# Loading x of the first four chunks one token per partition, with another order of steps

## The chip, the cores and the metric

The kernel runs on one core of one Trainium2 chip. The metric is the device time in microseconds of one execution; three executions of the kernel before took 118.48, 118.60 and 118.94 us (median 118.6). A profile of one execution shows the five engines: TensorE (PE; its weight loads are shown as PEld), VectorE (DVE), ScalarE (ACT), GpSimd (POOL) and SyncE (SP, which here only issues DMA transfers).

## What is computed

Two layers, one after the other. The first is a gated scan over a sequence (batch 4, heads H = 8, sequence S = 768, head size D = 32, state size N = 16); the second is a feed-forward layer with a GELU of the tanh form on the 3072 tokens of 256 values that the first gives (hidden size 2048). The reference of the first layer, cut to its core (its chunks are 32 long; the result doesn't depend on that):

```python
la = log_a[:, :, sl]; cum = np.cumsum(la, axis=-1)
L = np.exp(cum[:, :, :, None] - cum[:, :, None, :]) * causal
M = np.einsum('bhin,bhjn->bhij', Cc, Bc) * L
y_intra = np.einsum('bhij,bhjd->bhid', M, xc)
y_inter = np.einsum('bhin,bhnd->bhid', Cc, state) * np.exp(cum)[..., None]
y[:, :, sl] = y_intra + y_inter
decay_from_j = np.exp(cum[:, :, -1:] - cum)
Bx = np.einsum('bhjn,bhjd->bhjnd', Bc, xc) * decay_from_j[..., None, None]
state = np.exp(np.sum(la, axis=-1))[..., None, None] * state + np.sum(Bx, axis=2)
```

and of the second:

```python
x = attn_out.transpose(0, 2, 1, 3).reshape(B * S, H * D)
h = x @ w_in
g = 0.5 * h * (1 + np.tanh(np.sqrt(2 / np.pi) * (h + 0.044715 * h ** 3)))
out = g @ w_out
```

## The kernel before, in words

The sequence of each batch is cut into six chunks of 128 tokens, 24 in all; two chunks form a unit u (0 to 11), and a unit is also a tile of 256 tokens for the second layer. The kernel is a list of small named steps. Each step has an engine and a function that issues its instructions (`add`, L751); the string ORDERED (L17) lists all of them in the order in which they are issued. Each engine works through its own instructions in that order, so the list settles what stands behind what on every engine and on the DMA queues of SP and ACT. A letter after a colon picks the engine (A, D, P), `~n` issues n blocks of 128 columns of matmuls with zeros on TensorE (`fill`, L701), and `+n` puts n such blocks ahead of a step s1. Waits between engines follow from the data and from the buffers; every DMA transfer also waits for the transfer issued eight before it.

The steps that matter here, by name:

- Loads: load_aq and load_a (the gate a, once for the first four chunks of batch 0 and once for all), load_bc0 (C and B of the first four chunks, L149), load_bc1 (the last two of batch 0), load_bc (other batches), load_x.u (L171, two transfers of 128 KB, one token per partition: runs of 32 floats), load_wi.q and load_wo.q (quarters of the two weights, 512 KB each), and load_x4 (L182), which loads x of the first four chunks of batch 0 in one transfer with four successive tokens per partition.
- The gate: clipq, Rq (a scan), tpq, recip0, peq, ppq, pendq for the first four chunks; clip, R, tp2, tp6.q, recip, recip1, pe, pp, pend for all batches. They give the factors rt, pt and the decays pend.
- B and C: mulb and mulc multiply them by their factors, with four tokens per partition; tw.i transposes, ew copies the result back in token order as bh0 and ce0. For batch 1 that is mul, T, E, and F splits C by head; N turns B back to tokens on the partitions and bn copies it. Batches 2 and 3 go through DRAM instead (load_wr, load_tr, load_bn).
- x of units 0 and 1: with four tokens per partition it must be put back in token order. x4 casts it, XX (L563) multiplies it by a selection matrix unp (set up by c_unp) into the order of tokens, and xn copies the outcome. XD (L575) forms the products of B and x straight from the loaded order, r by r. Other units: castx.u casts x to bf16, and D.u multiplies B (bn) and x.
- Per unit: G.u (products of B and C), M.u.i (L612, times the mask, 1024 columns on VectorE; for unit 0 half of it as GE on ACT and ME on GpSimd), S (the state of a chunk), SP (the state spread over heads), Y.u (both parts of y, which needs M, x and SP), yev.u (copies y as the input of the second layer). From u = 3 on, Y.u also issues D and G of the next unit.
- The second layer: s1.u.i (eight steps a unit of four matmuls each, L708), gelu.u.i on ACT, s2.chunk.quarter (four steps a chunk of four matmuls each, L725), oev (copies the sum), store. wi.q.k and wo.q.k cast the loaded weights. s1 needs yev of its unit and w_in; s2 needs the gelu steps and w_out.

For unit 0 the list before runs: a, C and B of four chunks, x4, w_in; tw, ew, G.0, M.0.0, XX.0, XD.0, SP.0, Y.0, yev.0, and then the first s1 with unit 1's steps in between.

Of the kernel before, what the change touches and what calls it, by code (L numbers as in the profile page):

```python
# [8 lines left out]
FP32 = mybir.dt.float32  # L9
# [12 lines left out]
load_wi.2 SP.0 ~17 Y.0 wi.0.1:A wi.0.0:A S.0.0 yev.0.0.2 wi.1.1 XX.1 wi.1.0:A R XD.1 S.0.1
load_wi.3 S.1.0 s1.0.0 SP.1 xn.2 load_bc1.1 wi.2.0 gelu.0.0 G.1 s1.0.1 s1.0.2 M.1.1 M.1.0
load_bc1.0 load_wo.0 wi.3.0:D gelu.0.1 wi.2.1 s1.0.3 load_x.2 SP.2 pe wi.3.1 gelu.0.2 load_bc.1.1
gelu.0.3 tp6.2 s1.0.4 load_bc.1.0 gelu.0.4 load_x.3 load_wo.1 xn.3 s1.0.5 s1.0.6 Y.1 gelu.0.5 pp
tp2 gelu.0.6 tp6.3 recip1 s1.0.7 S.1.1 yev.1.0.2 mul1.0:P mul1.1:P tp6.1 pend gelu.0.7 s1.1.0
wo.0.1 T1.0 s1.1.1 T1.1 gelu.1.0 bh1 N1 gelu.1.1 s1.1.2 tp6.0 s1.1.3+10 bn1 ce1.1 load_wo.2
castx.2.None SP.3 wo.0.0 ce1.0 gelu.1.2 gelu.1.3 G.2 s1.1.4 recip.1.4 s1.1.5 gelu.1.4 M.2.1
mul.1.1:P s2.0.0.0.o D.2 M.2.0 load_x.4 gelu.1.5 s2.0.1.0.o s1.1.6 T.1.1 gelu.1.6 S.2.0 s1.1.7
# [954 lines left out]
```

## Time and profile before

| what | us |
|---|---|
| three runs | 118.48, 118.60, 118.94 |
| span of the profiled execution, first to last instruction | 116.9 |
| median of the runs less that span | 1.7 |
| TensorE busy | 110.1 |
| ScalarE busy | 72.1 |
| VectorE busy | 69.4 |
| GpSimd busy | 21.4 |
| start of the first s1 (L717) | 12.50 |
| last copy out (L323) starts | 113.91 |

The profile gives the span of the profiled execution; its own time outside the span isn't listed, so the median of the runs is set beside it. Busy times are sums over the whole span. TensorE is busy nearly throughout, but its matmuls with zeros (7.6 us in 23 instructions at L705) count as busy too. The granted TensorE clock is full in every slice. 15.97 MB move by DMA, and the DMA engines are nearly full from about 4 to 34 us and then have room.

### The profile page before, as it was taken

What the parts mean: (1) busy time and instruction counts of PE and PEld (TensorE: products, weight loads), DVE (VectorE), ACT (ScalarE), POOL (GpSimd) and SP (SyncE); (2) the same over time, 40 slices, a digit from 0 to 9 for tenths busy, and PEclk for the clock granted to TensorE, in tenths of its full rate; (3) what the DMA queues carried; (4) which work ended last, traced back from release to release, by engine and by line L of the source; (5) the groups of instructions that cost most, each with busy time, mean ns of one, the idle gap of its engine ahead of it and who ended that gap; (6) DMA issues with size and microseconds to landing.
All of it is one profiled execution on the core that took longest, in us unless ns stands there. A gap on an engine that the chain in (4) does not pass through costs nothing.

```text
span 116.9 us, 3379 instructions
## 1 busy us (share of the span) xinstructions
PE 110.1 (94%) x1426; PEld 92.0 (79%) x1426; DVE 69.4 (59%) x140; ACT 72.1 (62%) x139; POOL 21.4 (18%) x38
## 2 busy tenths in 40 slices
PE   6988999998899999999999999999999999999990
PEld 2354676776789979989898999889798998999970
DVE  5898899899785936716695583049493462101020
ACT  2249899968486459565766677828465587447501
POOL 7606816908206000052200000000000000000000
PEclk9999999999999999999999999999999999999999
DMA  0999997999983929998407472044201201101113
GB/s 26 228 332 357 281 252 178 208 288 257 305 143 90 185 47 219 213 253 200 72 25 171 121 163 63 0 140 98 40 6 63 71 0 52 43 0 50 45 47 132
DMA packets 43007, 15.97 MB, mean 137 GB/s; under 512 B 36657, under 2 KB 41457, under 8 KB 42993
## 3 DMA queue, kind: packets, MB, share of 16 engines
q1 hardware_dynamic: 42800, 15.64, 56.0%
q8 instruction: 11, 0.18, 0.6%
q10 hardware_dynamic: 192, 0.13, 0.5%
q14 instruction: 4, 0.02, 0.1%
HBM read 11.04 MB, written 3.93 MB: 128 GB/s over the span
## 4 chain that ended last, share of the span: by engine, by line
PE 75%; DMA 8%; DVE 6%; SPq 6%; issue 2%; POOL 1%; ACT 0%; DVEq 0%; POOLq 0%
PE o_ps L735 33%; PE hp L717 30%; DMA bcf<-in_B_dram 8%; PE yb L735 3%; SPq L190 3%; PE ga L603 3%; PE yb L658 2%; DVE m L613 2%; PE yb L667 2%; DVE ce L523 1%; SPq L150 1%; DVE bh L327 1%; DVE bc L484 1%; SPq L159 1%; SPq L183 1%
## 5 line engine op out<-in xcount | busy, mean ns | idle before, releaser
L721 ACT ACTIVATE gT<-hp 128x512 bf16<-128x512 f32 x96 | 54.3, 596 | 25.0 <-PE hp L717 24.6
L717 PE MATMUL hp<-xm,w_in_sb 128*128 128x256 bf16 x384 | 53.3, 273 | 0.6 <-ACT gT L721 0.4
L735 PE MATMUL o_ps<-w_out_sb,gT 128*128 128x256 bf16 x352 | 47.3, 273 | 0.0
L717 PEld LDWEIGHTS <-w_in_sb 128*128 128x128 bf16 x384 | 41.4, 114 | 3.5 <-issue 1.9
L735 PEld LDWEIGHTS <-gT 128*128 128x128 bf16 x384 | 37.0, 98 | 4.9 <-issue 1.1
L327 DVE COPY o_sb<-o_ps 128x256 f32<-128x256 f32 x13 | 5.5, 425 | 23.8 <-PE o_ps L735 20.4
L613 DVE TENSOR_TENSOR m<-ga,tri 128x1024 bf16<-128x1024 f32 x12 | 14.6, 1218 | 0.1
L613 DVE TENSOR_TENSOR m<-gb,tri 128x1024 bf16<-128x1024 f32 x11 | 13.4, 1219 | 0.7 <-PE gb L603 0.7
L323 ACT ACTIVATE o_sb<-o_ps 128x256 f32<-128x256 f32 x9 | 3.5, 385 | 9.2 <-PE o_ps L735 9.2
L705 PE MATMUL yb<-wz 128*128 128x512 bf16 (+3 forms) x23 | 7.6, 481 | 1.1 <-DVE wz L220 1.1
L691 DVE SCALAR_TENSOR_TENSOR sp_new<-s_new,pend,bmask 128x256 bf16<-128x256 f32 x17 | 7.9, 476 | 0.0
L327 DVE CAST xm<-yb 128x512 bf16<-128x512 f32 x6 | 4.1, 687 | 5.8 <-PE hp L636 4.8
L684 DVE SCALAR_TENSOR_TENSOR s_new<-s_new,pend,hp 128x64 f32<-128x64 f32 x13 | 3.6, 279 | 6.4 <-PE hp L636 6.2
L705 PEld LDWEIGHTS <-wz 128*128 128x128 bf16 x26 | 3.0, 120 | 5.1 <-issue 3.2
L667 PE MATMUL yb<-m,x 128*32 128x128 bf16 x192 | 6.1, 220 | 0.0
L603 PE MATMUL ga<-ce,bh 32*128 32x256 bf16 x48 | 4.7, 273 | 1.3 <-DVE bn L327 0.9
L484 POOL TENSOR_TENSOR bc<-bc_t,pt 128x768 bf16<-128x768 f32 x2 | 3.0, 1494 | 13.8 <-DMA bc_t<-in_C_dram 13.7
L658 PE MATMUL yb<-ce,sp_new 128*32 128x128 bf16 x160 | 5.3, 221 | 0.0
L603 PE MATMUL gb<-ce,bh 32*128 32x256 bf16 x48 | 4.7, 273 | 0.0
L735 PE MATMUL yb<-w_out_sb,gT 128*128 128x256 bf16 x32 | 4.6, 273 | 0.0
L667 PEld LDWEIGHTS <-x 128*32 128x32 bf16 x192 | 3.8, 97 | 0.8 <-issue 0.8
L323 ACT ACTIVATE xm<-yb 128x512 bf16<-128x512 f32 x6 | 3.6, 595 | 1.1 <-PE hp L636 1.1
(115 smaller groups left out, 79.5 us busy)
## 6 DMA issues: line engine op xcount, KB each, us to landing
out_dram<-o_sb SPq DMA_DIRECT2D x24, 128.0 KB, 1.9
x_t<-in_x_dram SPq DMA_DIRECT2D x20, 128.0 KB, 3.9
wf<-in_moe_w_in_dram SPq DMA_DIRECT2D x4, 512.0 KB, 6.7
wf<-in_moe_w_out_dram SPq DMA_DIRECT2D x4, 512.0 KB, 5.5
bc_t<-in_C_dram SPq DMA_DIRECT2D x3, 384.0 KB, 5.8
bc_t<-in_B_dram SPq DMA_DIRECT2D x3, 384.0 KB, 5.5
scr<-bc SPq DMA_DIRECT2D x4, 192.0 KB, 2.2
x_t<-in_x_dram SPq DMA_DIRECT2D x1, 512.0 KB, 5.8
```

What stands on the lines that cost most here:

```text
L323: nc.scalar.activation(o, i, AF.Copy)
L327: nc.vector.tensor_copy(out=o, in_=i)
L484: (nc.gpsimd if eng == "POOL" else nc.vector).tensor_tensor(out=d["bc16"][:, i], in0=d["bc"].rearrange("p i h (r n) -> p i r h n", r=R6)[: ...
L603: nc.tensor.matmul(out=gbank(g)[:, 256 * k:256 * k + 256], lhsT=bh_of(2 * u + k)[gs], rhs=ce_of(2 * u + k)[gs], start=True, stop=True, til ...
L613: nc.vector.tensor_tensor(out=m_of(u)[:, 2 * i:2 * i + 2].rearrange("p g k e t -> p (g k e) t"), in0=gx[i].rearrange("p g (k t) -> p (g k) ...
L658: nc.tensor.matmul(out=y4[32 * j:32 * j + 32, k, w], lhsT=sp[:, 32 * h:32 * h + 32], rhs=ce_of(gc)[:, h % 2], start=first(j), stop=False, ...
L667: nc.tensor.matmul(out=y4[32 * j:32 * j + 32, k, w], lhsT=X16[u][:, k, 32 * h:32 * h + 32], rhs=m[:, h // 2, h % 2, :], start=first(j), st ...
L691: nc.vector.scalar_tensor_tensor(out=sp_new.rearrange("p (g d) -> p g d", g=4), in0=(XN[0][:, H * D:H * D + 64] if gc == 0 else state[("s" ...
L705: nc.tensor.matmul(out=t[:, 0:m * 128], lhsT=wz, rhs=w3.to_broadcast([128, m, 128]), start=True, stop=True, skip_group_check=True)
L717: nc.tensor.matmul(out=hp[:, j * T:(j + 1) * T], lhsT=w_in_k[:, w, q, k], rhs=xm[:, w, u * T:(u + 1) * T], start=(w == 0), stop=(w == 1))
L721: nc.scalar.activation(gts[u][:, 2 * i:2 * i + 2], hps.pop((u, i)).rearrange("p (j t) -> p j t", j=2), AF.Gelu_apprx_tanh)
L735: nc.tensor.matmul(out=ops[gc], lhsT=gts[u][:, fi, k * Q:(k + 1) * Q], rhs=w_out_sb[:, fi, :], start=(fi == 0 and (u > 0 or k == 0)), stop ...
```

## The change

Units 0 and 1 are treated like the others. load_x4, x4, XX, XD, xn and c_unp with its selection matrix go. load_x gets an argument for the chunk, so each unit is two steps, load_x.u.0 and load_x.u.1, each of 128 KB, and units 0 and 1 are loaded by them too: load_x.0.0 and load_x.1.0 right behind C and B of four chunks, load_x.0.1 and load_x.1.1 behind the first quarter of w_in. castx.0.0, castx.0.1 and castx.1 cast them. B of the first four chunks is turned back by N0 (two transposes each, two steps) and copied by bn0, and D.0 and D.1 use it as D does for other units.

The list ORDERED is a new one throughout, found by a search in which the durations of the steps were disturbed. What differs near the start: both load_a come ahead of the table load on ACT; clip and R come ahead of mulb on VectorE, tp2 ahead of M.0.0; mulc.1 is on GpSimd; bn0.0 and ME.3 are on VectorE, ahead of SP.0; load_wo.1 to load_wo.3 come ahead of the second half of x of unit 2 and of B and C of batch 1; all eight s2 steps of unit 0 and four of unit 1 are issued ahead of G.3 and D.3, where the list before had two; there are more fillers (118 blocks by themselves ahead of the first s1 against 83, and 12, 5, 4 and 10 blocks as part of s1 steps against 10). A field `behind` on the steps is set but read by nothing in the kernel.

```diff
-    def load_x(u):
+    def load_x(u, k):
         b, c = divmod(2 * u, CPB)
-        XF[u] = ldx.tile([128, 2, H, D], FP32, name="x_t")
-        for k in range(2):
-            nc.sync.dma_start(out=XF[u][:, k], in_=x[b, :, (c + k) * Q:(c + k + 1) * Q, :]
-                              .rearrange("h p d -> p h d"))
...
-    def load_x4():
-        nc.sync.dma_start(out=x4_t, in_=x[0, :, 0:R4 * Q, :].rearrange("h (p r) d -> p h (r d)", r=R4))
+        if k == 0:
+            XF[u] = ldx.tile([128, 2, H, D], FP32, name="x_t")
+        nc.sync.dma_start(out=XF[u][:, k], in_=x[b, :, (c + k) * Q:(c + k + 1) * Q, :]
+                          .rearrange("h p d -> p h d"))
...
-    def c_unp():
...
+    def f_N0(k):
+        T0[("n", k)] = pso.tile([128, 512], FP32, name="o_ps").bitcast(BF16)[:, 0:256]
+        for c in range(2):
+            nc.tensor.transpose(out=T0[("n", k)][:, c * 128:(c + 1) * 128],
+                                in_=bh0[0][:, (2 * k + c) * Q:(2 * k + c + 1) * Q], identity=ident)
+
+    def f_bn0(k, eng):
+        copy(eng, bn0[0][:, 2 * k:2 * k + 2].rearrange("p c n -> p (c n)"), T0[("n", k)])
...
-    def f_XX(u):
...
-    def f_XD(u):
...
-    def f_xn(c, eng):
...
-        d = XN[gc][:, H * D:H * D + 64] if gc in XN else DT[u][:, 64 * k:64 * k + 64]
+        d = DT[u][:, 64 * k:64 * k + 64]
...
+    for k in range(2):
+        n0 = add("E", f_N0, k, deps=[bh[2 * k]])
+        bn[2 * k] = bn[2 * k + 1] = add("A", f_bn0, k, alt="AD", deps=[n0])
+        n0.takes("o", bn[2 * k])
...
-        if u < 2:
-            xx = add("E", f_XX, u, deps=xc4 + [cunp])
-            dn[u] = add("E", f_XD, u, deps=[xx, mulb])
-            xn[u] = [add("A", f_xn, c, alt="AD", deps=[xx]) for c in cs]
-        else:
...
+        xn[u] = [add("P", f_castx, u, k, alt="PAD", deps=[xl[(u, 0)] if k == 0 else xl[(u, 1)], Yn.get(u - 6), dn.get(u - 6)])
+                 for k in ((0, 1) if u == 0 else (None,))]
+        xl[(u, 0)].takes("xl", *xn[u])
+        dn[u] = add("E", f_D, u, deps=[bn[cs[0]]] + xn[u])
```

The new order, up to G.3 and D.3:

```diff
+c_wz c_cz load_aq.2 load_aq.0 c_ident load_aq.3 c_zero load_aq.1 c_sel ~59 load_a.1:A clipq Rq
+load_a.0:A c_warm tpq c_bmask load_bc0.1 load_bc0.0 recip0 clip R load_x.0.0 mulb mulc.0 mulc.1:P
+load_x.1.0 tw.0 tw.1 c_m4 peq c_tri c_m8 castx.0.0:D pe tw.2 ew.1.0:A ew.0.1 ew.0.0:A ~5 N0.1
+load_wi.0 ew.0.2 ~4 G.0 ew.1.1:A tp2 wi.0.0 ew.1.2 GE.2 bn0.1 ~17 ~16 ppq load_x.0.1 ~3 N0.0 M.0.0
+castx.0.1 load_x.1.1 GE.3 pp load_wi.1 pendq:D bn0.0:D ~3 G.1 D.0 pend:D load_wi.2 ME.3:D
+castx.1.None:A ME.2 SP.0 S.0.0 load_wi.3 ~2 ~1 ~11 Y.0 S.0.1 wi.0.1:D D.1 S.1.0 yev.0.0.2 S.1.1
+tp6.0 M.1.1 wi.1.1:A SP.2 wi.1.0 load_bc1.0 M.1.0 wi.2.0 wi.2.1 SP.1 load_wo.0 wi.3.0 load_bc1.1
+s1.0.0+12 gelu.0.0 s1.0.1 wi.3.1:D c_par gelu.0.1 mul1.0:P s1.0.2+5 gelu.0.2 s1.0.3 recip1 s1.0.4+4
+tp6.3 gelu.0.3 load_x.2.0 load_wo.1 wo.0.0:D s1.0.5 Y.1 gelu.0.4 s1.0.6 gelu.0.5 s1.0.7 wo.0.1
+yev.1.0.2 mul1.1:P tp6.2 tp6.1 wo.1.1 T1.0 s2.0.0.0.o gelu.0.6 load_wo.2 gelu.0.7 s1.1.0 T1.1 s1.1.1
+s2.0.1.0.o load_wo.3 ce1.0:D bh1 gelu.1.0 ce1.1:D gelu.1.1 recip.1.4 s1.1.2 G.2 wo.1.0:A M.2.0
+s1.1.3+10 wo.2.0:D M.2.1 s2.0.0.1.o s2.0.1.1.o load_x.2.1 wo.2.1 load_bc.1.0 gelu.1.3 gelu.1.2 N1
+wo.3.1:D wo.3.0:A s2.0.0.2.o s2.0.1.2.o s1.1.4 s2.0.0.3.o s2.0.1.3.o gelu.1.4 load_bc.1.1 bn1:D SP.3
+castx.2.None:D D.2 load_x.3.0 oev.1 s1.1.5 gelu.1.5 S.2.0 SP.4 mul.1.0 s1.1.6 Y.2 s1.1.7 oev.0 T.1.0
+mul.1.1:P E.1.0 s2.1.0.0.o gelu.1.6 s2.1.0.1.o yev.2.0.2 s1.2.0 N.1 gelu.1.7 load_x.4.0 gelu.2.0
+T.1.1 E.1.1:A bn.1:D s1.2.1 s2.1.0.2.o s1.2.2 s2.1.0.3.o load_x.5.0 load_x.3.1 F.1 castx.3.None:D
+gelu.2.1 gelu.2.2 s1.2.3 G.3 D.3 oev.2 s2.1.1.0.o S.3.0 S.3.1 gelu.2.3 M.3.0 M.3.1 SP.6 s1.2.4
```

156 lines of the change are left out of this document (52 added, 104 removed).

## The prediction

> **What bounds the kernel now.** I read the page first (span, engines, slices), then busy time by stages, then the chain of waits in order of time, and last the start of the span engine by engine. The page, and the busy time of four stretches (columns: stretch, length, then busy us and count for PE, PEld, DVE, ACT, POOL, then clock, DMA share, GB/s):
>
> ```profile
> span 116.9 us, 3379 instructions
> PE 110.1 (94%) x1426; PEld 92.0 (79%) x1426; DVE 69.4 (59%) x140; ACT 72.1 (62%) x139; POOL 21.4 (18%) x38
> ...
> 12.50:17.50 5.00, 4.60 (x68) 3.47 (x68) 4.55 (x10) 4.50 (x10) 2.12 (x4) 1.00 1.08 245
> 17.50:30.20 12.70, 11.25 (x154) 8.44 (x146) 11.44 (x21) 10.09 (x21) 7.71 (x11) 1.00 1.02 240
> 30.20:113.90 83.70, 83.67 (x1072) 75.00 (x1064) 43.43 (x76) 50.61 (x94) 4.73 (x4) 1.00 0.44 98
> 113.90:116.90 3.00, 0.00 (x0) 0.00 (x0) 0.00 (x0) 0.38 (x1) 0.00 (x0) 1.00 0.39 132
> ```
>
> From 30.2 us TensorE has no gap at all (83.67 of 83.70), and 3.0 us of copy and store follow. Nothing can be won there unless work is taken from TensorE. Ahead of it VectorE (11.44 of 12.70) and the DMA engines (share above 1) are full. The chain of waits (start, length, what):
>
> ```profile
> 22.24 2.36 DVE m L613 x2
> 24.60 0.20 DVE s_new L684
> 24.82 0.48 DVE sp_new L691
> 25.31 0.87 DVE bc L484
> 26.17 0.66 DVE xm L327
> 26.84 0.90 DVE bh L327
> 27.74 1.44 DVE ce L523 x2
> 29.17 0.48 DVE bn L327
> ...
> 30.26 0.56 PE hp L717 x4
> 30.82 0.44 PE o_ps L735 x4
> ```
>
> Before 30 us it runs on VectorE without a break, afterwards on TensorE: a step s1 or s2 of four matmuls takes 0.437 us. The timeline of the head fixes the start:
>
> ```profile
> 10.72 0.47 DVE L691 SCALAR_TENSOR_TENSOR sp_new<-o_ps,pendq,bmask 128x256 bf16<-128x256 f32 x1
> 11.24 0.94 DVE L340 TENSOR_TENSOR_SCAN r_t<-ac,ends 64x384 f32<-64x384 f32 x1
> ...
> 12.50 0.60 PE L717 MATMUL hp<-xm,w_in_sb 128*128 128x256 bf16 x4
> ```
>
> SP.0 ends at 11.19, Y.0 and its copy follow, s1.0.0 starts 1.31 us later. The scan over a for all batches comes after SP.0 and so costs s1.0.0 nothing.
>
> **The frame of the sum.** Three numbers decide: when s1.0.0 starts, when D.3 has run (from there TensorE was dense), and how many s1 and s2 steps are done by then. Before: 12.50 us; 30.2 us; s1.0, s1.1, s1.2.0 to 2 and two of s2.0, 21 steps. In the new order 32 steps stand ahead of D.3 (s1.0, s1.1, s1.2.0 to 3, all eight of s2.0, four of s2.1). Eleven more are 11 x 0.437 = 4.8 us of work that the dense part no longer has, so the kernels tie when D.3 ends at 35.0 us.
>
> **The change, part by part.**
>
> *x and B.* Out go sixteen matmuls and 64 small ones of x and D of units 0 and 1 (XX.0 and XD.0 fill 9.34 to 10.1, XX.1 and XD.1 11.6 to 12.4), the memset, reduction and four copies of unp on VectorE (3.32 to 4.25, 0.9 us) and the four copies xn. In come D.0 and D.1 (16 small matmuls, 0.2 us each as at 30.02), four transposes N0 (0.055 us each), two bn0 copies (0.42 as the like `bh<-o_ps`) and three casts. On TensorE that lies in time in which it waited or ran fillers; the value is in what waits next: D.0 now needs B turned twice (tw.0, copy, N0, copy) and M.0.0, ME.3, bn0.0 ahead of SP.0 on VectorE.
>
> *VectorE up to SP.0.* Both loads of a go ahead of the table load on ACT's queue, and clip and scan (0.34, 0.94) ahead of mulb. The loads of a took 2.9 to 3.8 us to land; issued at 1.74 and about 2.2, the last lands between 5.1 and 6.0, and I take 5.6. VectorE is free by then: unp's steps are gone, and tpq and recip0 end about 5.2. From 5.6 its new order is clip 0.34, scan 0.94, mulb 0.68, mulc 0.42, m4 0.19, peq 0.28, cast of half a unit 0.21, two of pe 0.33, a copy ce 0.41, tp2 4 x 0.235, M.0.0 1.22, pendq 0.17, bn0.0 0.42, pend 0.19, ME.3, SP.0 0.47. ME.3 has no row on VectorE; half of M is 0.61, the cast of the same width from SBUF 0.42 (a binary form can't be priced below it), and I take 0.6. Sum 7.8, so SP.0 ends at 13.4 instead of 11.19, and s1.0.0 starts at 13.4 + 1.31 = 14.7. Bounds: mulb can't start before B lands (2.19 + 4.2 = 6.4; I have 6.9), so 0.4 earlier at best, and 0.4 later with a at 6.0. **The start is 2.2 us later.**
>
> *From s1.0.0 to D.3.* TensorE's work there: 32 x 0.437 = 14.0, Y.1 and Y.2 1.1, G.2 and G.3 0.65, D.2 and D.3 0.3, transposes T1, N1, T.1, N.1 24 x 0.055 = 1.3, 19 filler blocks of 128 columns 1.05: 18.4, so D.3 can't end before 33.1. VectorE's chain in its new order: S.0.0, S.0.1, wi.0.1 0.87; S.1, tp6.0 1.05; M.1.1, SP.2, M.1.0, SP.1 3.4 (Y.1 may start at about 18.9); wi.3.1, par, recip1, tp6.3, wo.0.0, two tp6 2.9; two ce1 and recip 1.85; M.2.0, wo.2.0, M.2.1, wo.3.1 3.3; bn1, SP.3, castx.2, S.2.0, SP.4 2.1; mul.1.0, E.1.0, bn.1, F.1 4.0; castx.3 0.4. That is 19.9, from 13.4 to 33.3. In three places VectorE must wait for TensorE in between: castx.2, D.2, S.2.0 (0.4), mul.1.0, T.1.0, E.1.0 (0.6: in the old trace bc ends at 26.17 and the copy starts at 26.78) and E.1.0, N.1, bn.1 (0.55); small ones 0.15. So castx.3 ends at 35.0 and D.3 at 35.2. **That is 0.2 us past the tie.**
>
> How far do full durations overstate? Two M in a row start 1.14 apart though each lasts 1.22, so some 0.07 a row, 30 rows, about 2 us at best; TensorE's own 33.1 and the wait for Y.1 (TensorE is through with s1.0.5 at 18.2, Y.1 may start at 18.9) hold that gain to about 1.3. Against it stand waits that a sum of durations doesn't see. In the old trace both cancel: VectorE's durations from 12.63 to 29.63 add up to 17.2 in 17.0 us. I take zero.
>
> *Loads.* x at one token per partition moves runs of 128 bytes. Nearest row: the two bcf loads of 128 KB with such runs landed at 14.7 and 16.7 when the last w_in quarter was down at about 14.3, 1.0 to 1.2 us each; in single stretches late in the trace x and stores moved 150 to 173 GB/s, 0.85 us for 128 KB. The old x4 load (512 KB, runs of 512 bytes) took from 6.4 to 8.6, 2.2 us. Four loads take 3.4 to 4.7 us, so all that follows is 1.2 to 2.5 us later. At the slow end, with 1.4 us for each 512 KB of weights and 1.6 for 384 KB of B or C: w_in done at 16.7 (needed 18.9), w_out 3 at 25.9 (26.7), x.2 at 27.1 (28.0), B of batch 1 at 28.7 (29.5), C at 30.3, whose product, transposes and copy end at 33.4 where F.1 wants it at 33.0, and x.3 at 35.0 where castx.3 wants it at 34.5. So 0 at the fast end, up to 0.9 at the slow one; I take 0.4. Three more loads on SP's queue (0.4 to 0.65 us of issue each) stand ahead of w_in's third quarter; that queue is waiting for landings by then.
>
> *The dense part.* Its order is shuffled, but the steps are the same and F.2, F.3 stay some steps ahead of their Y; nothing there is priced, its cover being the backlog of s2. The last store is preceded by four filler blocks (0.2 us) that no copy waits for. Zero; if the cover fails, up to 2 us.
>
> **Sum.** 0.2 + 0 + 0.4 + 0 = 0.6 us. The page gives the span, 116.9, of one execution; the median of the three runs is 118.6, so 1.7 us lie around the span, unchanged. Forecast: span 117.5, **119.2 us**.
>
> **The rivals.**
> 1. *VectorE starts rows closer than their durations (faster).* The chain in its place would end D.3 at 33.9 instead of 35.2: with loads on time 118.6 - 1.1 = 117.5, with part of it 118.2. It decides once 0.6 us of the sum are saved. For it: L613's starts 1.14 us apart, and w_out cast early gives TensorE eight s2.0 steps in waits that the old order couldn't fill (17.7 us from 12.5 to 30.2 held 13.4 of work). Against: the tally 17.2 in 17.0.
> 2. *Loads become the bound (slower).* If 128-byte runs hold everything up by 2.5 us and VectorE also waits for w_out 3 and x.2, each in front of the whole chain: D.3 at about 37, 120.6. For it: DMA share above 1 through the whole head. Against: the needs above lie up to 2 us behind the landings.
> 3. *TensorE falls back to half rate.* The first fillers came every 0.427 us up to 5.73, then every 0.215. The old head never left TensorE idle over 0.6 us; now 59 blocks end at 6.6 and tw.0 waits until 7.6. A fallback would double some 2 us of work before Y.0: 121.2. The Trainium skill, page "TensorE: Matmul & The Clock Gate", section "Part 1: The HAM clock gate", says half rate comes back after an idle window of about 3.4 us; by that a gap of 1 us leaves the rate alone and the sum stays 119.2. No run shown here has such a gap, so the trace can't say.
> 4. *The dense part gets gaps* where a unit's Y waits for B or C through DRAM: 120.5.
>
> **How the numbers follow.** Forecast (118.8 to 119.9) 0.42; rival 1 0.33, of which 0.27 lie below 118.0; rival 2 0.15; rival 3 0.04; rival 4 0.06. About 0.5% (0.6 us) is what a measurement of this kernel can tell from no change: 118.0 to 119.2. Faster: those 0.27. Same: the other 0.06 of rival 1 and 0.16 of the forecast, 0.22. Slower: the other 0.26 of the forecast and rivals 2 to 4, 0.51. The range 117.4 to 120.9 leaves out the far ends of rivals 1 to 4, about 0.2.
>
> **What would show it.** s1.0.0 at 14.7 (14.2 to 15.2); Y.1 near 18.9; D.3 near 35.5 (tie 35.0); VectorE full from 6 to 35 us; last matmul near 114.5; x loads of 0.85 to 1.2 us one after the other; fillers at 0.215 after 6 us. Wrong if s1.0.0 comes before 14, if D.3 ends before 34.5 or after 36.5, or if TensorE has gaps after D.3.

## The result, and the profile after

The changed kernel is slower: 1.0128 times the kernel before, with a 95% interval of 1.008 to 1.0176, which is 120.1 us against 118.6 (four executions of the kernel before beside it: 118.48 to 118.94). In two of its four executions the granted TensorE clock averaged 0.986 and the span was 120.1 and 120.2 us; the ratio, and all that follows on the profile, is of the other two (119.95 and 120.59 us, spans 117.8 and 118.5).

The page of the changed kernel, and then the busy time of four stretches (columns as before: stretch, length, busy us and count for PE, PEld, DVE, ACT, POOL, clock, DMA share, GB/s):

```profile
span 117.8 us, 3297 instructions
PE 111.4 (95%) x1384; PEld 93.1 (79%) x1384; DVE 68.8 (58%) x138; ACT 71.9 (61%) x135; POOL 20.9 (18%) x37
```

```profile
13.00:19.00 6.00, 5.50 (x80) 3.73 (x73) 5.69 (x13) 3.29 (x6) 3.31 (x5) 1.00 1.11 339
19.00:35.00 16.00, 15.94 (x213) 13.57 (x210) 12.95 (x27) 12.22 (x24) 4.15 (x5) 1.00 0.97 227
35.00:114.80 79.80, 79.76 (x1040) 71.06 (x1037) 41.35 (x71) 51.38 (x96) 6.07 (x7) 1.00 0.43 100
114.80:117.80 3.00, 0.00 (x0) 0.00 (x0) 0.00 (x0) 0.16 (x1) 0.00 (x0) 1.00 0.14 46
```

The span is 0.9 us longer in these two single executions. (Executions of the kernel before differ by as much: in 57 of them beside the experiments, at a clock of 0.996 or more, the span is 115.8 to 117.5 us, with a median of 116.5. So a few tenths between two traces say little.) Behind 35 us TensorE is as dense as before (79.76 of 79.80), only shorter by the steps that now lie ahead. So the loss was made before D.3, and the timeline shows where (start, length, engine, line, what, and in brackets the idle time ahead of it and what ended it):

```profile
6.29 0.35 DVE L322 TENSOR_SCALAR ac<-a_t 64x384 f32<-64x384 f32 x1 [1.31 <-DMA a_t<-in_a_dram]
8.27 0.40 PE L419 MATMUL o_ps<-ident,bc0s 128*128 128x128 bf16 x4 [1.71 <-POOL m L249]
13.51 0.48 DVE L649 SCALAR_TENSOR_TENSOR sp_new<-hp,pendq,bmask 128x256 bf16<-128x256 f32 x1 [0.16 <-PE hp L594]
13.39 0.93 PE L663 MATMUL yb<-wz 128*128 128x256 bf16 x5
14.25 0.29 PE L625 MATMUL yb<-m,x 128*32 128x128 bf16 x8
...
15.47 1.03 PE L675 MATMUL hp<-xm,w_in_sb 128*128 128x256 bf16 x8
...
29.40 0.95 DVE L478 TENSOR_TENSOR bc<-bc_t,rt 128x768 bf16<-128x768 f32 x1
30.76 1.49 POOL L478 TENSOR_TENSOR bc<-bc_t,pt 128x768 bf16<-128x768 f32 x1 [5.52 <-DMA bc_t<-in_C_dram]
31.12 0.96 DVE L312 COPY bh<-ga 128x768 bf16<-128x768 bf16 x1 [0.76 <-PE ga L487]
32.76 0.56 DVE L312 COPY bn<-ga 128x768 bf16<-128x768 bf16 x1 [0.69 <-PE ga L523]
33.94 0.75 DVE L517 TENSOR_SCALAR ce<-ch,par 128x768 bf16<-128x768 bf16 x2 [0.62 <-ACT ch L308]
...
35.50 0.24 PE L594 MATMUL hp<-x,bn 128*32 128x64 bf16 x8
...
114.58 0.38 ACT L308 ACTIVATE o_sb<-o_ps 128x256 f32<-128x256 f32 x1 [1.36 <-PE o_ps L693]
```

The gate's clip (L322) waits for a until 6.29. TensorE's first transposes come at 8.27 after 1.71 us without work; what they read is mulb's outcome, which ended at 8.22 (the row names GpSimd's instruction that ended at the same moment). SP.0 ends at 13.99, Y.0 starts at 14.25, and s1.0.0 at 15.47 instead of 12.50. From 29.4 us VectorE takes three turns with other engines: it waits 0.76 for TensorE's transposes of B, 0.69 for the transposes back and 0.62 for ScalarE's copy of C. C's product on GpSimd (L478) had waited 5.52 us for its load. D.3 ends at 35.50 + 0.24 = 35.74, and the last copy out starts at 114.58, where before it started at 113.91.

The chain of waits of the changed kernel (start, length, what) over the same stretch:

```profile
23.12 0.81 DVE pt L376
23.93 0.46 issue
24.39 1.22 DVE m L571
25.62 0.35 DVE w_out_sb L312
26.00 1.03 PE o_ps L693 x8
...
35.24 0.21 PE ga L561 x2
35.57 0.17 PE hp L594 x8
35.74 0.54 PE o_ps L693 x4
```

Before, the chain ran on VectorE until 29.65 us. Now it passes to TensorE at 26.0: the eleven steps s1 and s2 that were pulled ahead of D.3 fill the waits, which TensorE could not fill before. The busy time from s1.0.0 to the end of D.3, before and after, shows the same:

```profile
12.50:30.26 17.76, 15.91 (x214) 11.97 (x215) 15.99 (x30) 14.58 (x30) 9.84 (x15) 1.00 1.04 241
15.47:35.74 20.27, 19.71 (x252) 16.34 (x251) 16.50 (x32) 15.60 (x30) 6.73 (x9) 1.00 1.01 238
```

Here TensorE is without work for 0.56 us, where it was for 1.85 before. VectorE's three turns now cost VectorE time, and TensorE next to none. With 19.71 us of busy time behind a start at 15.47, D.3 could not have ended before 35.18 even without any wait.

The frame of the prediction gives the tie at 30.26 + 4.81 = 35.07. D.3 came 0.67 us after it: the start is 2.97 us later and the stretch behind it 2.51 longer, and the eleven steps save 4.81. The last copy came 114.58 - 113.91 = 0.67 us later. The other 0.2 us of the span lie behind that copy (117.8 - 114.96 = 2.84 us, before 116.9 - 114.29 = 2.61).

### The profile page after: what moved, and what is told of

Its sections match the earlier page's. It is cut to its first block, busy times and chain, and to the rows that moved or that the text cites. A ratio compares the mean times of both kernels' runs of the same rounds, so it can differ in the third digit from the quotient of the medians.

```text
span 117.8 us, 3297 instructions
## 1 busy us (share of the span) xinstructions
PE 111.4 (95%) x1384; PEld 93.1 (79%) x1384; DVE 68.8 (58%) x138; ACT 71.9 (61%) x135; POOL 20.9 (18%) x37
## 4 chain that ended last, share of the span: by engine, by line
PE 86%; DMA 3%; DVE 3%; POOL 2%; ACT 1%; issue 1%; SPq 1%; POOLq 0%
PE hp L675 35%; PE o_ps L693 32%; PE yb L663 3%; PE ga L561 3%; PE yb L693 3%; DMA bcf<-in_C_dram 3%; PE yb L625 3%; PE yb L616 3%; PE hp L663 1%; POOL m L249 1%; DVE m L571 1%; ACT gT L679 1%; PE hp L594 1%; DVE ce L448 1%; DVE pt L376 1%
## 5 line engine op out<-in xcount | busy, mean ns | idle before, releaser
L675 PE MATMUL hp<-xm,w_in_sb 128*128 128x256 bf16 x384 | 54.1, 273 | 0.0
L693 PE MATMUL o_ps<-w_out_sb,gT 128*128 128x256 bf16 x352 | 47.9, 273 | 0.1
L312 DVE COPY o_sb<-o_ps 128x256 f32<-128x256 f32 x11 | 4.7, 425 | 15.8 <-PE o_ps L693 15.8
L571 DVE TENSOR_TENSOR m<-gb,tri 128x1024 bf16<-128x1024 f32 x11 | 13.4, 1214 | 0.0
L663 PE MATMUL yb<-wz 128*128 128x512 bf16 (+3 forms) x35 | 10.2, 431 | 1.1 <-DVE warm L216 1.1
L663 PEld LDWEIGHTS <-wz 128*128 128x128 bf16 x44 | 4.5, 114 | 6.2 <-issue 3.6
L649 DVE SCALAR_TENSOR_TENSOR sp_new<-s_new,pend,bmask 128x256 bf16<-128x256 f32 x17 | 8.7, 517 | 0.0
L310 POOL CAST x<-x_t 128x512 bf16<-128x512 f32 (+1 forms) x6 | 3.4, 576 | 22.7 <-DMA x_t<-in_x_dram 22.7
L308 ACT ACTIVATE xm<-yb 128x512 bf16<-128x512 f32 x9 | 5.4, 600 | 2.8 <-PE hp L594 2.8
L308 ACT ACTIVATE o_sb<-o_ps 128x256 f32<-128x256 f32 x11 | 4.2, 381 | 3.1 <-PE o_ps L693 2.0
L640 DVE COPY s_new<-hp 128x64 f32<-128x64 f32 x4 | 0.9, 222 | 7.7 <-PE hp L594 7.7
```

The lines of the kernel that those rows point to most:

```text
L308: nc.scalar.activation(o, i, AF.Copy)
L312: nc.vector.tensor_copy(out=o, in_=i)
L571: nc.vector.tensor_tensor(out=m_of(u)[:, 2 * i:2 * i + 2].rearrange("p g k e t -> p (g k e) t"), in0=gx[i].rearrange("p g (k t) -> p (g k) ...
L649: nc.vector.scalar_tensor_tensor(out=sp_new.rearrange("p (g d) -> p g d", g=4), in0=(DT[0][:, 0:64] if gc == 0 else state[("s", gc)]).rear ...
L663: nc.tensor.matmul(out=t[:, 0:m * 128], lhsT=wz, rhs=w3.to_broadcast([128, m, 128]), start=True, stop=True, skip_group_check=True)
L675: nc.tensor.matmul(out=hp[:, j * T:(j + 1) * T], lhsT=w_in_k[:, w, q, k], rhs=xm[:, w, u * T:(u + 1) * T], start=(w == 0), stop=(w == 1))
```

## The experiments

The table sets beside each run's ratio to the kernel before the times of its profiled execution. "Stretch" is from s1.0.0 to the end of D.3; "past tie" is the end of D.3 less 35.07 (less 30.26 for e8, whose list is the old one); "last copy" is the start of the last copy out less 113.91; "idle" is the time in the stretch in which the profile shows no work on TensorE. e1 has the old list with other steps, and its half rate (below) leaves no frame for it.

| run | ratio, 95% interval | s1.0.0 | D.3 ends | stretch | idle | past tie | last copy |
|---|---|---|---|---|---|---|---|
| changed kernel | 1.0128 [1.008, 1.0176] | 15.47 | 35.74 | 20.27 | 0.56 | +0.67 | +0.67 |
| e1_old_order | 1.084 [1.0771, 1.0909] | | | | | | |
| e2_long_runs | 1.0233 [1.0159, 1.0306] | 15.37 | 36.78 | 21.41 | 1.59 | +1.71 | +1.71 |
| e3_no_fill | 1.0207 [1.0114, 1.0301] | 13.90 | 35.51 | 21.61 | 1.40 | +0.44 | +0.84 |
| e4_gate_late | 1.041 [1.0283, 1.0536] | 17.52 | 40.01 | 22.49 | 1.26 | +4.94 | +4.93 |
| e5_long_c_first | 1.0195 [1.0133, 1.0257] | 16.01 | 36.76 | 20.75 | 1.01 | +1.69 | +1.95 |
| e6_long_f_first | 1.0205 [1.0146, 1.0263] | 15.66 | 36.69 | 21.03 | 1.35 | +1.62 | +1.61 |
| e7_more_fill | 1.0111 [1.0062, 1.016] | 15.34 | 35.96 | 20.62 | 0.82 | +0.89 | +0.89 |
| e8_before_bn_act | 1.008 [1.0047, 1.0112] | 12.81 | 31.11 | 18.30 | 2.40 | +0.85 | +1.07 |
| e9_early_long | 1.015 [1.0104, 1.0195] | 14.36 | 35.94 | 21.58 | 1.91 | +0.87 | +1.07 |
| e10_early_long_f | 1.0168 [1.0112, 1.0224] | 15.41 | 37.23 | 21.82 | 2.15 | +2.16 | +2.16 |
| e11_early | 1.0077 [1.0033, 1.0121] | 15.57 | 36.29 | 20.72 | 0.30 | +1.22 | +1.22 |
| e12_c_on_dve | 1.0097 [1.0063, 1.0132] | 14.24 | 34.51 | 20.27 | 0.61 | -0.56 | -0.56 |

The last two columns agree within 0.4 us in every run, and in eight of the eleven with the new list within 0.02: what D.3 loses, the end loses. In the runs with the new list, TensorE is busy for 19.66 to 20.21 us of the stretch (more only in e4 and e11, which have half rate in it), and the stretches differ mostly by what TensorE idles. Each row is one execution, and chance is in it too: the clip, which waits for a, started between 5.61 and 6.65 us in those that have it ahead of mulb.

e2, e5, e6, e9, e10 and e12 read the same number of bytes of x for units 0 and 1 in another order, so those values aren't the reference's.

**e1_old_order: the new x path under the old order.** Loads, casts, N0, bn0 and D stand in the places of load_x4, x4, XX, XD and xn; the rest of the list is the old one.

```diff
-... clipq load_x4 Rq tpq recip0 c_cz mulc.0 ~59 tw.1 ...
+... clipq load_x.0.0 load_x.0.1 load_x.1.0 load_x.1.1 Rq tpq recip0 c_cz mulc.0 ~59 tw.1 ...
-... pendq x4.0:P XX.0 ME.2 XD.0 GE.3 xn.1 ME.3 xn.0:D load_wi.2 SP.0 ...
+... pendq castx.0.0:A castx.0.1:P N0.0 bn0.0:D ME.2 D.0 GE.3 ME.3 load_wi.2 SP.0 ...
-... wi.1.1 XX.1 wi.1.0:A R XD.1 S.0.1 ...
+... wi.1.1 N0.1 bn0.1:A wi.1.0:A R castx.1.None:P D.1 S.0.1 ...
```

> The old list of steps, with only the steps of x and B of units 0 and 1 exchanged: load_x4 becomes four loads of 128 KB in its place, XX.0 and XD.0 become N0.0, bn0.0 and D.0, XX.1 and XD.1 become N0.1, bn0.1, castx.1 and D.1. Theory (the short runs of x cost, the new list was found for them): all four loads stand ahead of w_in, so w_in and everything behind lands 1.2 to 2.5 us later, TensorE waits for it, and the time is 119.8 to 121.5, above that of the changed kernel or level with it. Rival (the new list itself is what costs, the new x path is nearly free): 118.6 to 119.2.

It took 128.3 us, well beyond that. The timeline has TensorE waiting 1.04 us for bn0 ahead of D.0 and 2.36 us for a cast of x ahead of D.1; from then on the busy time by stretches has half the clock:

```profile
11.38 0.24 PE L593 MATMUL hp<-x,bn 128*32 128x64 bf16 x8 [1.04 <-DVE bn L311]
15.68 0.24 PE L593 MATMUL hp<-x,bn 128*32 128x64 bf16 x8 [2.36 <-POOL x L309]
```

```profile
18.00:21.00 3.00, 1.63 (x8) 0.97 (x7) 2.87 (x8) 1.19 (x2) 0.00 (x0) 0.50 0.98 230
...
24.00:27.00 3.00, 3.00 (x42) 2.06 (x41) 0.00 (x0) 1.44 (x3) 0.93 (x2) 0.50 1.09 229
```

So the new x path needs another list than the old one: in these places of it the casts and copies stand late on their engines, and TensorE waits for them. Rival 3's mechanism, which no trace had shown, exists.

**e2_long_runs: the same bytes in runs of 1 KB.**

```diff
     def load_x(u, k):
+        if u < 2:   # 128 tokens of 256 values, one run each
+            nc.sync.dma_start(out=XF[u][:, k]..., in_=bass.AP(... ap=[[H * D, Q], [1, H * D]]))
+            return
```

> The changed kernel, but the four loads of x of units 0 and 1 read 128 KB in runs of 1 KB instead of 128 bytes, from contiguous memory (the tokens land in another order, so the values of units 0 and 1 are not the reference's; all else is computed as before). Theory (loads hold the chain through C of batch 1, whose product ended at 32.25 us, and F.1 at 33.94, which waited 0.6 us): everything behind lands some 2 us earlier, F.1 starts 0.6 us earlier, D.3 ends at about 35.1 instead of 35.7, ratio to the kernel before about 1.006. Rival (VectorE's own chain is the bound whatever the loads do): D.3 within 0.2 us of 35.7, ratio 1.010 to 1.015.

All later loads came earlier, C's product at 29.25 instead of 30.76; but s1.0.0 stayed at 15.37 and D.3 came a whole microsecond later. The timeline shows why: C's product on GpSimd now falls on B's product on VectorE, and that takes 2.27 us instead of 0.95.

```profile
29.25 1.49 POOL L483 TENSOR_TENSOR bc<-bc_t,pt 128x768 bf16<-128x768 f32 x1 [5.06 <-DMA bc_t<-in_C_dram]
29.29 2.27 DVE L483 TENSOR_TENSOR bc<-bc_t,rt 128x768 bf16<-128x768 f32 x1
```

Loads in short runs do delay what follows. What the delay costs by itself this run can't say, since the earlier C cost VectorE 1.3 us.

**e3_no_fill: without the filler blocks ahead of ppq and Y.0.**

```diff
-... bn0.1 ~17 ~16 ppq load_x.0.1 ...
+... bn0.1 ppq load_x.0.1 ...
-... S.0.0 load_wi.3 ~2 ~1 ~11 Y.0 ...
+... S.0.0 load_wi.3 Y.0 ...
```

> The changed kernel without the 33 filler blocks ahead of ppq and the 14 ahead of Y.0. Theory (the fillers lie on the path: SP.0 ended at 13.99 and Y.0 started at 14.25 behind them, pendq waited 0.23 us for ppq): s1.0.0 starts 0.3 to 0.5 us earlier, at 15.0 to 15.2, but D.3 gains 0 to 0.3 us of it, ratio 1.009 to 1.013. Rival (without fillers TensorE falls back to half rate, since it idles about 2 us before Y.0): first s1 steps take 0.87 us each instead of 0.44, D.3 1 to 2 us later, ratio 1.02 to 1.03.

s1.0.0 came 1.57 us earlier, D.3 only 0.23. Not all of the 1.57 is the fillers' price: in this execution the clip started at 5.61, 0.68 us earlier than in the changed kernel. (The ratio holds two executions with a clock of 0.985 and 0.986 and one, the profiled, with 3.5 us outside its span; the two spans at full clock, 117.9 us both, are about those of the changed kernel.) VectorE's turn with ScalarE grew, because C's product still waited for its load (timeline):

```profile
30.77 1.49 POOL L478 TENSOR_TENSOR bc<-bc_t,pt 128x768 bf16<-128x768 f32 x1 [5.89 <-DMA bc_t<-in_C_dram]
...
33.71 0.75 DVE L517 TENSOR_SCALAR ce<-ch,par 128x768 bf16<-128x768 bf16 x2 [1.02 <-ACT ch L308]
```

With an earlier start the loads are the limit; with earlier loads alone (e2) the start and the stretched row on VectorE were.

**e4_gate_late: clip, R, pe, tp2, pp and pend behind S.1.1**, the old side of Y.0.

```diff
-... recip0 clip R load_x.0.0 ... castx.0.0:D pe tw.2 ... ew.1.1:A tp2 wi.0.0 ... GE.3 pp load_wi.1 ... D.0 pend:D ...
+... recip0 load_x.0.0 ... castx.0.0:D tw.2 ... ew.1.1:A wi.0.0 ... GE.3 load_wi.1 ... D.0 ...
-... S.1.1 tp6.0 ...
+... S.1.1 clip R pe tp2 pp pend:D tp6.0 ...
```

> The changed kernel with clip, R, pe, tp2, pp and pend moved behind S.1.1, so that VectorE needn't wait for a (idle 1.31 us before clip) nor scan it ahead of mulb. mulb then starts at about 6.45 instead of 7.56 and SP.0 comes 1.1 + 1.0 + 0.5 us earlier: s1.0.0 at 12.9 to 13.4. Theory of VectorE's chain (its idle 1.31 us is won back): Y.1 and D.3 come about 1 us earlier, D.3 at 34.7, ratio 1.003. Rival of the loads (C of batch 1 sets F.1): D.3 stays at 35.4 to 35.7, ratio 1.010 to 1.013, and the early start is lost again.

SP.0 ended about 1.2 us earlier, but in this place pp stands ahead of s1.0.0 on TensorE and waits for pe:

```profile
16.66 0.37 PE L387 MATMUL hp<-pe,selp 128*128 128x24 f32 x2 [3.08 <-DVE pe L381]
```

The granted clock was 0.50 from 18 to 21 us. The run tells nothing on the gate's price; it shows again that TensorE can lose its rate after some 3 us without work. It need not: three of the four executions had a mean clock of 0.986, the fourth, with the same list, 1.000.

**e5_long_c_first: e2 with C of batch 1 loaded ahead of B.**

```diff
-... wo.2.1 load_bc.1.0 gelu.1.3 ... gelu.1.4 load_bc.1.1 bn1:D ...
+... wo.2.1 load_bc.1.1 gelu.1.3 ... gelu.1.4 load_bc.1.0 bn1:D ...
```

> The run with 1 KB runs of x (its values of units 0 and 1 are again not the reference's), and load_bc.1.1 (C of batch 1) ahead of load_bc.1.0 (B). In the run before, GpSimd's product of C (29.25 to 30.74 us) met VectorE's product of B, which took 2.27 instead of 0.95 us. With C first, GpSimd is through by about 28.9 and VectorE's product takes 0.95 again. Theory (VectorE's chain with its three turns over TensorE sets D.3, loads don't): D.3 at 35.3 to 35.7, ratio 1.008 to 1.013, no better than the changed kernel although everything loads 1 to 2 us earlier. Rival (loads set it): D.3 at 35.1 or before, ratio up to 1.006.

B's product took 0.95 us again and the three turns were 0.77, 0.69 and 0.62 as in the changed kernel. s1.0.0 came at 16.01 in this execution. But the product of the next C ran into F.1, whose first half took 1.17 us instead of 0.41:

```profile
34.10 1.50 POOL L483 TENSOR_TENSOR bc<-bc_t,pt 128x768 bf16<-128x768 f32 x1 [0.97 <-DMA bc_t<-in_C_dram]
34.63 1.17 DVE L522 TENSOR_SCALAR ce<-ch,par 128x768 bf16<-128x768 bf16 x1 [0.62 <-ACT ch L313]
```

**e6_long_f_first: e5 with F.1 ahead of E.1.0**, and N.1 and bn.1 behind s1.2.1.

```diff
-... T.1.0 mul.1.1:P E.1.0 ... s1.2.0 N.1 ... T.1.1 E.1.1:A bn.1:D s1.2.1 ... F.1 castx.3.None:D ...
+... bn1:D mul.1.1:P ... D.2 T.1.1 E.1.1:A ... T.1.0 F.1 E.1.0 load_x.3.1 castx.3.None:D ... s1.2.0 ... s1.2.1 N.1 bn.1:D ...
```

> As the run before it, and in the list T.1.1 and E.1.1 behind D.2, F.1 ahead of E.1.0 on VectorE, castx.3 behind E.1.0, N.1 and bn.1 behind s1.2.1: VectorE then does F.1 while it would wait for T.1.0, N.1 and E.1.1 (idle 0.76, 0.69 and 0.62 us in the changed kernel). Theory (the turns of VectorE over TensorE set D.3): D.3 ends at 34.1 to 34.6, below the tie at 35.0, ratio 0.997 to 1.003. Rival (TensorE's own 18.4 us of work or the loads hold it): D.3 at 35.0 or later, ratio 1.006 or more.

F.1 came 3 us earlier (30.96 against 33.94) and its turn of 0.62 went, but D.3 hardly moved: VectorE was through with bn.1 at 35.04 and waited 1.71 us for D.3, where it waits 0.78 in the changed kernel.

```profile
30.96 0.74 DVE L522 TENSOR_SCALAR ce<-ch,par 128x768 bf16<-128x768 bf16 x2
...
36.74 0.22 DVE L645 COPY s_new<-hp 128x64 f32<-128x64 f32 x1 [1.71 <-PE hp L599]
```

VectorE's turns are not the limit here: TensorE has to get through the 32 steps (busy for 19.68 of the 21.03 us). Of what it idled, 0.57 us were for a cast of w_out that met GpSimd's product of C (the table at the end has it).

**e7_more_fill: 79 instead of 59 blocks at the start.**

```diff
-... load_aq.1 c_sel ~59 load_a.1:A clipq ...
+... load_aq.1 c_sel ~79 load_a.1:A clipq ...
```

> The changed kernel with 79 instead of 59 filler blocks at the start, so that TensorE is busy until about 7.7 us instead of 6.6, with tw.0 at 8.27. Theory (the granted clock of 0.986 over the span that some executions of the changed kernel show comes from TensorE idling there for 1.7 us): the granted clock is 1.000 in all executions, s1.0.0 stays at 15.4, D.3 at 35.7, ratio 1.010 to 1.014. Rival (it comes from another wait): executions at 0.986 still occur.

The wait ahead of TensorE's first transposes went from 1.71 to 0.35 us, s1.0.0 and D.3 stayed within 0.25 us of where they were, and all four executions had a clock of 0.999 to 1.000 and spans of 117.7 to 118.0.

```profile
8.14 0.40 PE L419 MATMUL o_ps<-ident,bc0s 128*128 128x128 bf16 x4 [0.35 <-POOL m L249]
```

Two of four executions of the changed kernel had the lower clock, none of four here. That doesn't show the gap as the cause. Of the 20 executions of the lists with such a gap, 1.40 to 1.96 us (changed kernel, e2, e3, e5, e6), 6 had a clock of 0.985 or 0.986, none of them in e6, whose gap is the longest; in e9 to e12, which have the 79 blocks but not those that e3 takes away, the clock was 0.983 to 0.986 in 8 of 36.

**e8_before_bn_act: the kernel before with bn.1 on ScalarE**, to take 0.5 us from the VectorE chain that the prediction found there.

```diff
-... N.1 gelu.2.0 F.1 s1.2.2 bn.1:D G.3 ...
+... N.1 bn.1:A gelu.2.0 F.1 s1.2.2 G.3 ...
```

> The kernel before with one change: bn.1 is copied by ACT right behind N.1 instead of by VectorE behind F.1. In its trace G.3 waited 0.89 us for bn.1. Theory (VectorE's chain sets D.3 there too): G.3 starts when F.1 ends, D.3 0.4 to 0.6 us earlier, ratio 0.995 to 0.997. Rival (ACT's copy of 0.8 us holds up gelu, and TensorE waits for its buffers instead): D.3 within 0.2 us of 30.2, ratio 0.998 to 1.003.

It was slower. On ScalarE the copy stands ahead of the gelu steps, and TensorE waited 1.39 us for a gelu (timeline):

```profile
28.66 0.81 ACT L321 ACTIVATE bn<-ga 128x768 bf16<-128x768 bf16 x1 [0.96 <-PE ga L527]
...
30.01 0.60 PE L715 MATMUL hp<-xm,w_in_sb 128*128 128x256 bf16 x4 [1.39 <-ACT gT L719]
```

s1.0.0 was 0.31 us later in this execution, D.3 0.85. So in the kernel before, too, a relief of VectorE alone was no gain: what VectorE is spared in this place, ScalarE pays at once, and TensorE waits for ScalarE.

**e9_early_long: the reliefs together**, e3, e5 and e7 in one list.

> All reliefs tried one by one, together: x of units 0 and 1 in runs of 1 KB, C of batch 1 loaded ahead of B, no filler blocks ahead of ppq and Y.0, and 79 instead of 59 blocks at the start. Theory (chain, loads and TensorE's own work stand level, so each relief alone ran into the next): taken together they add up. s1.0.0 near 13.9 as in the run without filler blocks, and from there the 19.7 to 20.2 us that the changed kernel and the run with C first took to G.3, so G.3 at 33.6 to 34.1 and D.3 at about 34.4, 0.7 before the tie of 35.07: span 116.0 to 116.6, time 118.0 to 118.6, no slower than the kernel before. Rival (something else that none of these touch, TensorE's waits for gelu or VectorE's three turns, sets D.3 by a fixed time): D.3 at 35.5 or later as in each of the single runs, 119.5 to 120.5.

1.015: the rival's time. Yet the rows say that the theory failed for a cause that neither had named. VectorE was 1.1 us ahead of the changed kernel at SP.3, and lost it in one row, again beside C's product on GpSimd:

```profile
26.45 1.49 POOL L483 TENSOR_TENSOR bc<-bc_t,pt 128x768 bf16<-128x768 f32 x1 [2.98 <-DVE w_out_sb L317]
...
26.44 1.78 DVE L654 SCALAR_TENSOR_TENSOR sp_new<-s_new,pend,bmask 128x256 bf16<-128x256 f32 x1
```

That row took 0.48 in the changed kernel. TensorE idled for 1.91 us of the stretch, 1.36 of them in one gap ahead of D.2, which waited for VectorE's next row, the cast of x.

**e10_early_long_f: e9 with the order of e6.**

> The same with the order in which F.1 stands ahead of E.1.0 and bn.1 at the end. Theory: VectorE's turns cost nothing as long as TensorE has s1 and s2 steps to run, so D.3 within 0.3 us of the run beside it, near 34.4, 118.0 to 118.8. Rival (the three turns of VectorE, 2.0 us in sum, set D.3 once the start is early): D.3 1 us or more earlier than in the run beside it, 117.0 to 117.6.

1.0168, which isn't told apart from e9's 1.015. In the profiled execution a came later (s1.0.0 at 15.41), and the same product fell on a cast of w_out, 1.73 us instead of 0.42 (VectorE at 25.48, GpSimd from 25.43 to 26.92), for which s2 then waited 1.38. So it says nothing about the turns: the row that GpSimd holds up is in both runs.

**e11_early: e3 and e7 with the short runs.**

> The changed kernel with its x loads and its order of loads, without the filler blocks ahead of ppq and Y.0 and with 79 blocks at the start. Theory: loads in runs of 128 bytes bring C of batch 1 at 30.7 and w_out's quarters late whatever the start, so s1.0.0 near 13.9 but F.1 waits for C as before and D.3 ends at 35.4: 119.2 to 119.8, 1 us more than the run with long runs. Rival (C isn't what held that run): as fast as the run with long runs.

1.0077, about 119.3: the time that the theory expected, and under the changed kernel's 1.0128, though the intervals overlap and the median of all its twelve executions is 120.3. And e9, which was to be 1 us faster, wasn't faster (120.4 in the same way). That fits a late product of C being cheaper than an early one that VectorE has to stand still for. Its profiled execution isn't the one to read D.3 from: it has a clock of 0.986 in the whole, and half rate in one place, which the busy time by single microseconds shows:

```profile
13.00:14.00 1.00, 0.74 (x32) 0.43 (x25) 0.96 (x5) 0.00 (x0) 0.46 (x1) 0.89 1.05 408
14.00:15.00 1.00, 1.00 (x22) 0.50 (x13) 0.96 (x5) 0.68 (x2) 0.25 (x2) 0.50 1.03 387
15.00:16.00 1.00, 1.00 (x5) 0.45 (x4) 1.00 (x3) 0.44 (x1) 1.00 (x2) 0.50 1.15 282
16.00:17.00 1.00, 1.00 (x6) 0.75 (x5) 1.00 (x2) 0.33 (x1) 0.66 (x2) 0.50 1.10 396
17.00:18.00 1.00, 1.00 (x9) 0.72 (x8) 1.00 (x2) 0.83 (x2) 0.72 (x2) 0.91 1.22 265
```

The clock lost 0.11 + 3 x 0.5 + 0.09 = 1.70 us in these five rows, and 118.3 x (1 - 0.986) = 1.66: a mean of 0.986 is one spell of half rate of 3.4 us. TensorE had no gap over 0.5 us there.

**e12_c_on_dve: e9 with C's product of batch 1 on VectorE.**

```diff
-... oev.0 T.1.0 mul.1.1:P E.1.0 ...
+... oev.0 T.1.0 mul.1.1 E.1.0 ...
```

> The run with all reliefs together, and C's product of batch 1 (unit's mul.1.1) moved from GpSimd to VectorE, behind B's product, in the 0.77 us that VectorE waits there for TensorE's transposes of B. (x of units 0 and 1 is read in another order, as in that run, so their values aren't the reference's.) Theory (a VectorE operation on SBUF can't run while GpSimd's product of C runs; this costs 1.3 us wherever the product falls): SP.3, which took 1.78 us there, takes 0.48 again, VectorE's rows behind it come 1.2 to 1.3 us earlier with respect to s1.0.0, the added product costs 0.1 to 0.2, and D.3 ends at about 34.8 instead of 35.94 (20.4 to 20.6 us after s1.0.0, in place of 21.6): time 1.0 to 1.2 us under that run, 119.0 to 119.4. Rival (the stretched row was only slack, and VectorE's turns or TensorE's steps set D.3): D.3 at 35.7 or later, the same time as that run within 0.4 us.

```profile
26.32 0.47 DVE L654 SCALAR_TENSOR_TENSOR sp_new<-s_new,pend,bmask 128x256 bf16<-128x256 f32 x1
...
29.03 0.95 DVE L483 TENSOR_TENSOR bc<-bc_t,pt 128x768 bf16<-128x768 f32 x1
...
34.27 0.24 PE L599 MATMUL hp<-x,bn 128*32 128x64 bf16 x8
```

SP.3 took 0.47, the product fitted into the wait for the transposes, and D.3 ended at 34.51, 20.27 us after s1.0.0 in place of 21.58. TensorE was as busy as in e9 (19.66 us, there 19.67); what went is its idle time, 0.61 us in place of 1.91. The last copy started 1.63 us earlier than in e9, and 0.56 earlier than in the kernel before. The time gained less, 1.0097 against 1.015, for the span of this execution was still 118.1: its last store took 3.3 us to land, where that of e9 took 1.7, and beside it the DMA view has one packet of instructions. The view of the DMA queues from 113.5 us on:

```profile
q8 instruction: 1, 0.02, 1.9%
...
out_dram<-o_sb SPq DMA_DIRECT2D x1, 128.0 KB, 3.3
```

Other executions of e12 at a clock near 1.0 had spans from 116.8 to 118.1; whether it is that packet which parts them stays open. So the four reliefs and one product on another engine bring the dense part to where the kernel before has it, not the whole time, and only with an x that isn't laid out so in memory. No kernel here beats the one before.

## Why the prediction was right

The direction and the frame came out: forecast 119.2 us with a range to 120.9, measured 120.1. Of the size, 0.6 us were forecast and 1.5 measured. That D.3 came within 0.24 us of its forecast (35.74, forecast 35.5) is luck: the start missed by 0.77 us, the stretch behind it by 0.53 the other way.

- **The frame** held best. A tie at 35.0 (35.07 worked out here) and "last matmul near 114.5" were read off: 114.54. The table bears it out over eleven lists.
- **VectorE up to SP.0** was mis-sized by its first term. The second load of a, issued at 2.21, landed at 6.20, after 4.0 us where the old trace had 2.9 and 3.8; that is outside the bounds of 5.1 to 6.0, and the clip started at 6.29 instead of 5.6. From there to the end of SP.0 it took 7.7 us, forecast 7.8. Behind that the 14 filler blocks ahead of Y.0 (the row at 13.39) had not been counted, which held it for 0.25. s1.0.0 came at 15.47, forecast 14.7 with 14.2 to 15.2.
- **TensorE from s1.0.0 to D.3** was mis-sized most, and the sum didn't feel it: 18.4 us of work were forecast, and it was busy for 19.71. The same prices gave 13.4 for the old stretch, where the prediction's own rows show 4.60 + 11.25 = 15.85. So TensorE's floor is 15.47 + 19.71 = 35.18 and not 33.1, and it is TensorE, not VectorE's chain as the sum had it, that sets D.3 once s1.0.0 has started.
- **VectorE from SP.0 to castx.3** took 35.0 - 14.0 = 21.0 us, forecast 21.6. That isn't rival 1 (rows closer than their durations): rows overlap by 1.3 us in 17.8 before and by 1.4 in 20.3 now, the same share. It is mostly one row. The prediction took F.1 from the old trace, where it took 1.52 us beside two casts on GpSimd; in the changed kernel nothing stands beside it, and it takes 0.75 (so mul.1.0, E.1.0, bn.1 and F.1, put down as 4.0, took 3.2). The rows of the kernel before:

```profile
27.65 1.52 DVE L523 TENSOR_SCALAR ce<-ch,par 128x768 bf16<-128x768 bf16 x2
27.67 1.29 POOL L325 CAST w_out_sb<-wf 128x512 bf16<-128x512 f32 x2 [0.23 <-DMA wf<-in_moe_w_out_dram]
```

- **The turns** were foreseen as 0.6 and 0.55 and came as 0.76 and 0.69; the third, 0.62 ahead of F.1, stood in the sum only as part of the loads' price.
- **Loads** came at the slow end that the prediction had worked out, or behind it: the last cast of w_in that waits for its load starts at 16.75 (16.7), the cast of w_out 3 at 26.77 (25.9, and ScalarE waited 0.72 for it), C's product at 30.76 (30.3). No run shows their price, 0.4 us in the sum, by itself. e2 shows that earlier loads can cost more than they bring: the late C fell by chance beside a copy from PSUM (VectorE's `bh<-ga`, 0.96 us in its usual length), and an earlier one falls on a row that must stand still.
- **The dense part** at zero was right; rival 4 did not come.
- **Rival 2** (loads the bound) is true only as one of three: e3 meets it at once, e2 and e5 do not.
- **Rival 3** was priced at 2.0 us and given 4 in 100. Its price was right, 120.15 - 118.15 = 2.0 us of span between the two pairs of executions, but it came in two of four. What starts it isn't known: the gap was 1.71 us and not near 1, since a came late and with it mulb, which ended at 8.22 instead of 7.6; but e11 has such a spell without a gap.
- **The tail.** The term for what lies around the span, 1.7 us, was 2.15 in the profiled execution (119.95 - 117.8). About half of the difference is an error of the sum: it set the median time beside the span of another execution, and in 58 executions of the kernel before the two differ by 1.78 to 2.10 us, with a median of 1.93. Of the 0.75 us between that execution and the forecast, 0.45 are this, 0.23 lie behind the last copy, and 0.07 is D.3 (0.67 past the tie, forecast 0.6).

Two things stay open: the gate's own price (e4 was to measure it and made a wait of its own), and a part of the 1.5 us themselves: 0.67 us ahead of the end of D.3, 0.2 behind the last copy and about 0.2 outside the span are found, about 0.4 are not, and two single traces can't settle so little.

## What to carry to other kernels

Where several engines and the loads end close to each other at the point that sets the end, a relief of one is worth next to nothing by itself: find that point, work out how late it may come (here D.3 and the eleven steps), look at which engine has no wait left ahead of it (here TensorE, with 0.56 us of 20.27), and test reliefs together before giving one up. Before loading something earlier, look at what its consumer will then run beside; a VectorE row on SBUF that begins just behind the start of a product on GpSimd stands still for almost the whole product. A row's time taken from an old trace can hold such a standstill: look at what stood beside it there. A gap in TensorE's work has two prices, the gap and the half rate that may follow, and the second shows in some executions only, so read the granted clock of each.

## What the runs showed of the hardware

**VectorE stands still while GpSimd multiplies.** In the five traces below a VectorE row on SBUF began within 0.9 us behind the start of GpSimd's product of 768 columns (in e9 0.01 us ahead of it). The product took its usual 1.49 us, and the row ended shortly after it, whatever its own length:

| run | VectorE row, usual | took | GpSimd ended | row ended |
|---|---|---|---|---|
| e2 | product of B, 0.95 | 2.27 | 30.74 | 31.56 |
| e5 | half of F.1, 0.41 | 1.17 | 35.60 | 35.80 |
| e6 | cast of w_out, 0.42 | 0.93 | 26.38 | 26.66 |
| e9 | SP.3, 0.48 | 1.78 | 27.94 | 28.22 |
| e10 | cast of w_out, 0.42 | 1.73 | 26.92 | 27.21 |

Casts on GpSimd do the same: F.1 in the kernel before (above), and in the changed kernel SP.2, 0.81 us from 16.98, beside a cast from 16.75 to 17.53. Where VectorE began well ahead, GpSimd was the one held up: in the kernel before, a product of 768 columns took 2.01 us from 35.28 beside VectorE's product from 34.99 to 35.94, and in e11 1.68 from 30.57 beside one from 29.95 to 30.90. VectorE's rows that read PSUM, such as the copy at 31.12 in the changed kernel, were not held up. The Trainium skill, page "SBUF — State Buffer", section "Who interferes with whom", says that VectorE and GpSimd share one pair of SBUF ports, and that it is an exclusive lock. The traces agree: the five rows end 0.20 to 0.82 us after GpSimd, and GpSimd isn't slowed in them.

**Half rate after less than a full idle spell.** Gaps of 2.36 and 3.08 us (e1, e4) were followed by a clock of 0.50 in the profile, but one execution of e4 kept its full clock; in the changed kernel, with one of 1.71, two of four executions have a mean clock that fits one such spell, in e3, with 1.89, as many, though not the profiled one, and in e6, with 1.96, none; in e11 no gap over 0.5 us was needed. Mean clocks of 0.986, 0.959, 0.946 and 0.933 (e4, e1) over spans of 122 to 127 us are losses of 1.7, 5.2, 6.8 and 8.5 us: one, three, four and five such spells. The Trainium skill, page "TensorE: Matmul & The Clock Gate", section "Part 1: The HAM clock gate", has a free-running window of about 3.4 us; the 3.4 us of half rate in e11 agree with its length. A whole idle window, after which half rate comes back in the rule that the prediction cites from that page, was not needed in e1, e4 and e11; what share of one has to be idle stays open.

**A packet of instructions late in the program** (0.02 MB) stood beside a last store that took 3.3 us to land instead of 1.7 in e12, and beside the one before the last in the changed kernel, where it cost nothing.
